# Linear attention with an ELU MLP on one core: the loads of chunks 12 and 13 placed behind the decay work of chunks 10 and 11, and three second products placed between the first products of chunk 8

## The chip, the core and the metric

The kernel runs on one core of one Trainium2 chip. The metric is device time in microseconds (us). Three runs of the kernel before gave 218.0, 218.4 and 217.15 us, so the median is 218.0 us.

The engines are TensorE (PE in the profile, PEld for its weight loads), VectorE (DVE), ScalarE (ACT), GpSimd (POOL) and SyncE (SP). DMAs in this kernel are issued from two queues: POOL issues the input loads, which turn float32 in memory into float16 on chip, and SP issues the transposes and the stores of the result. Both kinds of transfer run on the same 16 DMA engines of the core.

## The reference

There are two parts. The first is causal linear attention with a decay for each head, on q, k, v of shape 4 x 8 x 768 x 64 (batch, heads, tokens, head size), computed block after block with a state that is carried on:

```
intra = (qb @ kb^T * Dmask) @ vb                  # inside the block, masked with lam^(i-j)
inter = (qb * lam^(i+1)) @ kv_state               # from the blocks before
out   = intra + inter
kv_state = lam^block * kv_state + (kb * lam^(block-1-j))^T @ vb
```

The result is laid out as x of 3072 tokens x 512. The second part is an MLP: `h = x @ w_in` (512 x 2048), `g = h if h > 0 else exp(min(h, 0)) - 1`, `y = g @ w_out` (2048 x 512). The output y is float32.

## The kernel before

**Chunks.** The kernel uses blocks of 128 tokens instead of the reference's 64. A chunk is 128 tokens of one batch; there are 24, and chunk g belongs to batch g mod 4 and block g div 4. Chunks 0 to 3 go through the MLP one at a time, the others in pairs (4 and 5, 6 and 7, and so on). Everything that belongs to a pair is named by its first chunk: first product 1:8:j works on chunks 8 and 9 together.

**The steps of a chunk**, by the letters that the written-out order uses:

- `L` (load_pair, line 509) issues three loads on POOL's queue for a pair, in the order q, k, v (line 97). The tiles have four buffers.
- `W` (pool_work, line 513) issues two DMA transposes on SP's queue, q first and k second (line 256, from chunk 8 on; the tiles qT and kT have five buffers). It also does the decay work on POOL: kd, the decayed keys (line 162), and two halves of stt, the old state times its decay (line 366), for which the state update of four chunks earlier must have ended.
- `T` is the transpose on TensorE that chunks 0 to 7 use.
- `S` computes the scores psS on TensorE from kT and qT (line 290), 8 matmuls a chunk; VectorE then multiplies by the mask (pp, line 306).
- `B` is a burst on TensorE for a pair: P, the attention output psO (lines 326 and 332), and U, the addition to the state psU (line 394). VectorE or ScalarE copies the output out as xt (line 349 or 347), and VectorE updates the state st (line 406).
- `1:g:j` is a first product of the MLP, 8 matmuls into one of two psH buffers (line 466). ScalarE computes e = exp(psH) (line 472) and relu in place (line 473), and VectorE joins them as g (line 445). When that join has ended, the psH buffer is free.
- `2:g:j` is a second product, 4 matmuls into psM (line 488). After the fourth one of a chunk, ScalarE copies psM to osb (line 503) and SP's queue stores it (line 438).

**The order.** Nothing is scheduled by a planner: each engine runs its instructions in the order in which the program emits them, and each queue issues its transfers in that order. The emission order is the string OPEN (line 51) for the first part. From the point where OPEN ends, the loop at line 593 goes on by itself: it puts a first product, then the attention steps that are due by the table AT (line 61), then up to two second products that are ready. Any step that OPEN already holds is left out of the loop, so a longer OPEN takes work out of the loop and puts it elsewhere; nothing is done twice.

The VectorE join of a first product is not emitted directly behind it but at the start of the next first or second product (flush, line 440), and one waiting piece of VectorE work (a mask multiplication, a copy, a state update) is emitted behind each flush.

The stores of finished chunks are emitted at the start of first products, and one is kept back each time (line 457). A store waits on SP for its copy, and transposes that come later in SP's order stand behind it.

Of the kernel before, what the change touches and what calls it, by code (L numbers as in the profile page):

```python
# [15 lines left out]
def kernel(  # L16
# [13 lines left out]
    B, H, S, D = q.shape  # L30
# [23 lines left out]
        "2:1:2 1:1:3 U1 1:2:3 M Z3 2:2:2 1:3:2 U2 1:3:1 2:1:3 1:0:3 T5 T4 2:2:3 1:3:3 S4:5 "  # L54
        "2:0:3 2:3:2 2:3:0 M U3 M B:P4:P5:U4:U5 W8 2:3:3 1:4:1 T6 W9 1:4:0 T7 2:3:1 1:4:3 S6:7 "
        "1:4:2 2:4:0 2:5:0 1:4:5 1:4:4 2:4:1 B:P6:P7:U6:U7 1:4:7 1:6:1 2:5:2 2:5:1 1:6:0 1:4:6 "
        "2:4:2 S8:9 1:6:2 1:6:3 2:4:3 2:5:3 L12 1:6:4 B:P8:P9:U8:U9 1:6:5 W11 1:6:6 2:6:0 "
        "2:6:1 W10 1:6:7 2:6:2"
    )
    LAGU = 7  # L60
    AT = {"L": -18, "W": -13, "T": -9, "S": -8, "B": -4}
# [577 lines left out]
```

## Time and profile before

| | |
|---|---|
| median of three runs | 218.0 us (217.15 to 218.4) |
| span of the profiled execution | 215.9 us |
| TensorE busy | 199.9 us, 93% of the span |
| VectorE, ScalarE, GpSimd busy | 129.9, 129.1, 96.2 us |
| input and weight loads (POOL's queue) | 79760 packets, 13.50 MB |
| transposes and stores (SP's queue) | 22192 packets, 10.76 MB |

The whole time of the profiled execution itself is not given beside its span. The span is 2.1 us below the median of the three runs, and 1.2 to 2.5 us below single runs.

How to read it: a "busy" share says how long an engine had something to do, not whether it set the end. The "chain that ended last" goes back from the last instruction, at each step to whatever released it. The list of waits says which engine stood still, for whom, how long in all, how many times, and the longest. A timeline line gives the start, the busy time, the engine, the line of the kernel, the operation and tiles, how many instructions were merged, and in square brackets the idle time ahead of them and what ended it. "SPq" in a timeline is the issue on SP's queue; the time from issue to landing is in the DMA view, as the last number of a line.

### The profile page before, as it was taken

To read this page: it belongs to the slowest core of one execution; us is meant where nothing else is said; L and a number is where in the kernel's file an instruction comes from. 1 tells how busy PE (TensorE), PEld (TensorE's weight loads), DVE (VectorE), ACT (ScalarE), POOL (GpSimd) and SP (SyncE) were. 2 spreads that over 40 slices of the span, in tenths; PEclk is the share of its full clock that TensorE was granted. 3 is DMA by queue.
4 is the path that set the end of the run, shared out by engine and by line. 5 is a ranking of instruction groups with operands and counts; after the bars stand their busy time and mean duration, and the time that the engine had idled before them with its cause. 6 is when DMAs were issued, how large, how long until landed. Compare 5 with 4: busy or idle time off the path is not lost.

```text
span 215.9 us, 5095 instructions
## 1 busy us (share of the span) xinstructions
PE 199.9 (93%) x2036; PEld 138.2 (64%) x2036; DVE 129.9 (60%) x223; ACT 129.1 (60%) x245; POOL 96.2 (45%) x115
## 2 busy tenths in 40 slices
PE   0568999999999998999999999999999999999992
PEld 0466676768685675666766766766766666766641
DVE  3926463777837778658657657667667547444410
ACT  4536664884866656665565566476476576566730
POOL 7998890999996419167067159300000000000000
PEclk9999999999999999999999999999999999999999
DMA  8999999999999956989969919999114110111021
GB/s 89 140 173 193 190 144 180 139 169 144 151 156 145 143 126 131 123 109 97 153 114 125 175 58 103 152 181 152 50 59 90 52 49 0 55 49 49 3 92 54
DMA packets 101976, 24.59 MB, mean 114 GB/s; under 512 B 92608, under 2 KB 99008, under 8 KB 101952
## 3 DMA queue, kind: packets, MB, share of 16 engines
q0 software_dynamic: 79760, 13.50, 82.6%
q1 hardware_dynamic: 22192, 10.76, 25.6%
q8 instruction: 16, 0.26, 0.5%
q14 instruction: 8, 0.07, 0.1%
HBM read 27.27 MB, written 6.29 MB: 155 GB/s over the span
## 4 chain that ended last, share of the span: by engine, by line
PE 83%; DMA 7%; POOL 6%; issue 1%; DVE 1%; ACT 0%; SPq 0%; POOLq 0%
PE psM L488 38%; PE psH L466 36%; DMA wo<-in_moe_w_out_dram 4%; DMA kT<-kn 3%; PE psO L326 3%; PE psS L290 3%; PE psO L332 2%; POOL wi L136 1%; POOL kn L97 1%; POOL vn L97 1%; POOL qn L97 1%; PE psT L271 1%; PE psU L394 1%; POOL kd L162 0%; POOL wo L143 0%
## 5 line engine op out<-in xcount | busy, mean ns | idle before, releaser
L466 PE MATMUL psH<-xt,wi 128*128 128x256 f16 (+1 forms) x896 | 99.9, 259 | 1.5 <-DVE g L445 0.8
L445 DVE SCALAR_TENSOR_TENSOR g<-e,psH 128x512 f16<-128x512 f32 x96 | 65.8, 686 | 56.5 <-ACT psH L473 55.9
L488 PE MATMUL psM<-wo,g 128*128 128x512 f16 (+1 forms) x388 | 96.4, 377 | 0.9 <-DVE osb L501 0.5
L472 ACT ACTIVATE e<-psH 128x512 f32<-128x512 f32 x96 | 57.3, 597 | 66.1 <-PE psH L466 62.8
L466 PEld LDWEIGHTS <-wi 128*128 128x128 f16 x896 | 77.8, 99 | 26.8 <-DVE g L445 2.0
L473 ACT ACTIVATE psH<-psH 128x512 f32<-128x512 f32 x96 | 57.0, 594 | 0.0
L488 PEld LDWEIGHTS <-g 128*128 128x128 f16 x388 | 36.3, 98 | 29.9 <-issue 1.3
L306 DVE TENSOR_TENSOR pp<-psS,mask 128x512 f16<-128x512 f32 x48 | 30.9, 684 | 5.3 <-PE psS L290 5.3
L162 POOL TENSOR_TENSOR kd<-kn,ks 128x512 f16<-128x512 f16 x20 | 20.7, 1039 | 18.7 <-DMA kn<-in_k_dram 17.7
L366 POOL TENSOR_TENSOR stt<-st,upp 64x256 f32<-64x256 f16 x32 | 19.5, 608 | 19.8 <-DVE st L406 13.5
L503 ACT COPY osb<-psM 128x512 f32<-128x512 f32 (+1 forms) x24 | 13.9, 581 | 6.3 <-PE psM L488 6.3
L97 POOL DMA_DIRECT2D kn<-in_k_dram x14 | 15.5, 1106 | 0.8 <-POOLq L623 0.8
L97 POOL DMA_DIRECT2D vn<-in_v_dram x14 | 15.5, 1109 | 0.6 <-DMA wi<-in_moe_w_in_dram 0.6
L326 PE MATMUL psO<-pp,vn 128*64 128x128 f16 x192 | 12.4, 230 | 3.0 <-DMA vn<-in_v_dram 2.9
L97 POOL DMA_DIRECT2D qn<-in_q_dram x13 | 14.8, 1139 | 0.0
L406 DVE TENSOR_TENSOR st<-stt,psU 64x256 f16<-64x256 f32 x32 | 13.3, 417 | 1.2 <-PE psU L394 0.5
L326 PEld LDWEIGHTS <-vn 128*64 128x64 f16 x192 | 10.1, 114 | 6.1 <-DMA vn<-in_v_dram 3.1
L349 DVE TENSOR_TENSOR xt<-psO,qs 128x512 f16<-128x512 f32 x16 | 11.0, 688 | 4.1 <-PE psO L332 4.1
L332 PE MATMUL psO<-qT,st 128*64 128x128 f16 x160 | 10.0, 219 | 0.0
L271 PE MATMUL psT<-ident,qn 128*128 128x128 f16 x32 | 3.8, 252 | 6.5 <-DVE qn L115 5.6
L290 PE MATMUL psS<-qT,kT 64*128 64x128 f16 x192 | 8.7, 228 | 0.8 <-DMA kT<-kn 0.7
L332 PEld LDWEIGHTS <-st 128*64 128x64 f16 x160 | 8.9, 110 | 0.0
(38 smaller groups left out, 64.8 us busy)
## 6 DMA issues: line engine op xcount, KB each, us to landing
out_dram<-osb SPq DMA_DIRECT2D x23, 256.0 KB, 2.5
kn<-in_k_dram POOLq DMA_DIRECT2D x10, 256.0 KB, 8.1
qn<-in_q_dram POOLq DMA_DIRECT2D x10, 256.0 KB, 7.1
vn<-in_v_dram POOLq DMA_DIRECT2D x10, 256.0 KB, 8.6
wi<-in_moe_w_in_dram POOLq DMA_DIRECT2D x8, 256.0 KB, 7.4
wo<-in_moe_w_out_dram POOLq DMA_DIRECT2D x8, 256.0 KB, 8.4
kn<-in_k_dram POOLq DMA_DIRECT2D x4, 128.0 KB, 4.3
vn<-in_v_dram POOLq DMA_DIRECT2D x4, 128.0 KB, 6.1
```

The costliest lines, as they stand in the source:

```text
L97: nc.gpsimd.dma_start(out=t[:].rearrange("p b h d -> p (b h) d"), in_=src)
L162: nc.gpsimd.tensor_tensor(out=kd[:], in0=of(kg, g), in1=ks[:].unsqueeze(2).broadcast_to([128, H, 64]), op=ALU.mult,)
L290: nc.tensor.matmul(psS[g][hh][:, hp, :], lhsT=kt[r, hp, :], rhs=qt[r, hp, :], start=True, stop=True,)
L306: nc.vector.tensor_tensor(out=P[:], in0=pts[hh][:], in1=mask[:, hh::2, :], op=ALU.mult)
L326: nc.tensor.matmul(po[r, hp, :], lhsT=vt[:, 2 * hp + hh, :], rhs=Pt[(g, hh)][:, hp, :], start=True, stop=(cb == 0), skip_group_check=True,)
L332: nc.tensor.matmul(po[r, hp, :], lhsT=st[b][cb % 2][:, hp, r], rhs=qt[:, hp, :], start=False, stop=True, skip_group_check=True,)
L366: nc.gpsimd.tensor_tensor(out=tmp[r], in0=old[r, :, r], in1=upp[r].unsqueeze(2).broadcast_to([64, NHP, 64]), op=ALU.mult,)
L445: nc.vector.scalar_tensor_tensor(out=g[:].rearrange("p f c t -> p (f c t)"), in0=e[:], scalar=-1.0, in1=r[:], op0=ALU.add, op1=ALU.min,)
L466: nc.tensor.matmul(pH[:, f * n * 128 : (f + 1) * n * 128], lhsT=wi16[i][:, kk, w * 128 : (w + 1) * 128], rhs=xg[g0][:, kk, :], start=(kk = ...
L472: nc.scalar.activation(e[:], pH[:], AF.Exp)
L473: nc.scalar.activation(pH[:], pH[:], AF.Relu)
L488: nc.tensor.matmul(psM[g][:, cols], lhsT=gts[(g, j * FB + f)], rhs=wo16[i][:, w, cols], start=first and f == 0, stop=end and f == FB - 1, ...
```

## The change

The order string OPEN gets another end. `L12`, the three loads for chunks 12 and 13, moves from before 1:6:4 to behind `W10`. The string is also longer by seven steps, which the loop had placed before: 1:8:0, S10:11, 2:6:3, 1:8:1, 2:7:0, 1:8:2 and 2:7:1.

```
-        "2:4:2 S8:9 1:6:2 1:6:3 2:4:3 2:5:3 L12 1:6:4 B:P8:P9:U8:U9 1:6:5 W11 1:6:6 2:6:0 "
-        "2:6:1 W10 1:6:7 2:6:2"
+        "2:4:2 S8:9 1:6:2 1:6:3 2:4:3 2:5:3 1:6:4 B:P8:P9:U8:U9 1:6:5 W11 1:6:6 2:6:0 "
+        "2:6:1 W10 L12 1:6:7 2:6:2 1:8:0 S10:11 2:6:3 1:8:1 2:7:0 1:8:2 2:7:1"
```

With the part that the loop adds, the order of the stretch is, before and after (up to 1:8:7; all that follows is the same in both):

```
before: 2:5:3 L12 1:6:4 B8:9 1:6:5 W11 1:6:6 2:6:0 2:6:1 W10 1:6:7 2:6:2 1:8:0 S10:11
        1:8:1 1:8:2 2:6:3 1:8:3 W12 2:7:0 1:8:4 B10:11 2:7:1 1:8:5 W13 2:7:2 1:8:6 L14 2:7:3 1:8:7
after:  2:5:3 1:6:4 B8:9 1:6:5 W11 1:6:6 2:6:0 2:6:1 W10 L12 1:6:7 2:6:2 1:8:0 S10:11
        2:6:3 1:8:1 2:7:0 1:8:2 2:7:1 1:8:3 W12 1:8:4 B10:11 1:8:5 W13 2:7:2 1:8:6 L14 2:7:3 1:8:7
```

On POOL's queue this puts the loads of q, k, v behind kd and stt of chunks 11 and 10, where they stood ahead of them. On SP's queue the order of transposes and stores of chunks up to 13 stays as it was. On VectorE the second mask multiplication of chunk 11 and the join of 1:8:1 change places. On ScalarE the copy of chunk 6's result stands ahead of the exponential of 1:8:1, where it stood behind the relu of 1:8:2.

## The prediction

> **What bounds the kernel now.** I read the shares of busy time first, then the chain that ended last, then TensorE's timeline around the edit, then the timelines of the two queues.
>
> ```profile
> PE 199.9 (93%) x2036; PEld 138.2 (64%) x2036; DVE 129.9 (60%) x223; ACT 129.1 (60%) x245; POOL 96.2 (45%) x115
> ...
> PEclk9999999999999999999999999999999999999999
> ...
> PE 83%; DMA 7%; POOL 6%; issue 1%; DVE 1%; ACT 0%; SPq 0%; POOLq 0%
> ```
>
> TensorE sets the end, at a granted clock that stays in the top tenth. From 70 us on it is nearly never idle, so a change of order can only win what is left of idle time there. Its timeline shows two gaps in the stretch that the edit touches:
>
> ```profile
> 69.26 0.40 PE L290 MATMUL psS<-qT,kT 64*128 64x128 f16 x8
> 70.35 0.40 PE L290 MATMUL psS<-qT,kT 64*128 64x128 f16 x8 [0.70 <-DMA kT<-kn]
> ...
> 82.59 0.62 PE L290 MATMUL psS<-qT,kT 64*128 64x128 f16 x16
> 83.14 1.05 PE L466 MATMUL psH<-xt,wi 128*128 128x256 f16 x8
> 84.96 1.05 PE L466 MATMUL psH<-xt,wi 128*128 128x256 f16 x8 [0.77 <-DVE g L445]
> 85.85 1.03 PE L488 MATMUL psM<-wo,g 128*128 128x512 f16 x4
> ```
>
> The first gap is S9 waiting for the transpose kT9. The second is 1:8:2 waiting for a psH buffer, that of 1:8:0, whose join stands on VectorE behind two mask multiplications of S10:11. The edit aims at both. Now the queues, POOL first and then SP:
>
> ```profile
> 62.02 1.21 POOL L97 DMA_DIRECT2D qn<-in_q_dram  x1
> ...
> 65.58 1.04 POOL L162 TENSOR_TENSOR kd<-kn,ks 128x512 f16<-128x512 f16 x1
> 68.07 1.29 POOL L366 TENSOR_TENSOR stt<-st,upp 64x256 f32<-64x256 f16 x2 [1.45 <-DVE st L406]
> 69.44 1.04 POOL L162 TENSOR_TENSOR kd<-kn,ks 128x512 f16<-128x512 f16 x1
> 70.44 1.29 POOL L366 TENSOR_TENSOR stt<-st,upp 64x256 f32<-64x256 f16 x2
> ```
>
> ```profile
> 64.93 9.86 SPq L438 DMA_DIRECT2D out_dram<-osb  x3
> 74.96 1.23 SPq L256 DMA_TRANSPOSE qT<-qn  x1
> 76.28 1.22 SPq L256 DMA_TRANSPOSE kT<-kn  x1
> 77.61 1.21 SPq L256 DMA_TRANSPOSE qT<-qn  x1
> 78.87 1.26 SPq L256 DMA_TRANSPOSE kT<-kn  x1
> ```
>
> The last four are chunk 11's and then chunk 10's transposes, held back by a store that waits for ScalarE's copy (73.83). The line to watch is kT10, issued last at 78.87 and needed by S10 at 82.6. What a transpose takes from issue to landing is in the DMA view; first the answer for 74.8 to 79 us, with no loads in flight, then one for 101.4 us, amid the loads of chunk 16:
>
> ```profile
> qT<-qn SPq DMA_TRANSPOSE x2, 2.4
> kT<-kn SPq DMA_TRANSPOSE x2, 2.5
> ```
>
> ```profile
> vn<-in_v_dram POOLq DMA_DIRECT2D x1, 256.0 KB, 10.2
> kT<-kn SPq DMA_TRANSPOSE x1, 7.7
> ```
>
> So a transpose lands in 2.4 us alone, and in about 7 among loads. Transposes issued beside loads, from about 1 us after the first load of a group, read: kT9 6.9, kT13 7.0, qT15 7.8, kT15 7.7, qT17 6.4, kT17 6.9, qT19 7.2, kT19 7.7; median 7.1.
>
> **The change, part by part.**
>
> *S9's wait goes.* S8 starts at 69.26 and eight matmuls of this kind take 0.28 (16 of them take 0.55 at 82.59), so S9 could start at 69.54; it starts at 70.35: 0.81 us lost. kT9 was issued at 63.45, among L12's loads (62.02 to 65.5), and took 6.9. Without them the only other transfers are stores; an earlier transpose, kT8 at 59.29, took 4.5 with the tail of older loads beside it. At 4.5 kT9 lands at 67.95, ahead of the need. Next late for S9 would be qT9, issued before it. Gain 0.81; the bounds are 0 (kT9 still late) and 0.81. I take 0.81.
>
> *1:8:2's wait goes.* 1:8:1 starts at 83.14 and takes 0.87 in the chain, so 1:8:2 could start at 84.01 but starts at 84.96: 0.95. With 2:6:3 ahead of 1:8:1 and 2:7:0 behind it, two second products of 0.86 each lie between, more than the wait. Gain 0.95, and the second products only change place, so TensorE's work stays the same.
>
> *A new wait at 1:8:4.* Those second products now lack further on: 1:8:2, 2:7:1, 1:8:3, 1:8:4 follow one another. A psH buffer comes free 3.0 us after its product began (1:8:2 began at 84.96, its join ran 87.23 to 87.92, and a released product starts 0.04 later). 1:8:4 comes 0.87 + 0.86 + 0.87 = 2.60 behind 1:8:2 and needs its buffer: 0.38 lost. Its bounds are 0 (were the buffer free 13% sooner) and 0.95, the like wait of before; the chain from product to join is the same three steps, so I take 0.38. 1:8:5 follows the burst of 1.3 us, so it is covered; if the cover went, it would miss by the same 0.4.
>
> *L12 behind W10.* On POOL, kd11 now runs in the place of the loads, but stt11 still waits for VectorE's state update until 68.07; kd10 and stt10 follow and end at 71.73. So L12 is issued from 71.7 to 75.2 instead of 62.0 to 65.5. SP's queue: the store's copy comes 0.81 earlier, so qT11, kT11, qT10, kT10 are issued from 74.15, 75.45, 76.8 and 78.05, all inside L12's transfer (qT10 takes the buffer of qT8, which P8 reads until about 75, so that holds nothing up). A group's last load landed 10.8 to 12.7 us after the group's first issue (v14 86.21 + 8.5 against 83.87; v20 132.19 + 10.4 against 129.86): L12 is in flight until 82.5 to 84.4. S10 is reached at 82.66 - 0.81 = 81.85.
>
> When does kT10 land? Alone 78.05 + 2.4 = 80.5, so no wait; at the worst row, 78.05 + 7.8 = 85.85, a wait of 4.0. No row has a transpose issued so late in a load group, with three others ahead on its queue. The median row gives 85.15; the drain of the loads at its latest gives 84.4. I take 84.7, between them, as the loads thin out near the end: S10 waits 2.85 us. S11's transposes were issued earlier, and are no longer late by then. DVE's mask work behind S10 starts later with it, but TensorE is the one late.
>
> *Queued behind.* kd12 now waits for kn12 (71.7 + 1.2 + 8.0 = 80.9; it ran at 71.81), then stt12, kd13, stt13 (4.7 us in all) put L14 at 85.6 to 86.5 instead of 83.87. SP's kT12 waits for the same load instead of going at 82.22; with 7.8 for each landing, kT13 is there by 95, against S12 at 97.7. L14's two us pass on to kd14 (92.97 before) and L16 (98.01), and end in the next group, where POOL waited 1.95 for VectorE. No cost: the cover is that kd14 and kd15 are used only in the burst at 105; without it each us there is one on TensorE.
>
> **Sum:** -0.81 - 0.95 + 0.38 + 2.85 = +1.47 us. The profiled span of 215.9 becomes 217.4; around it lie 2.1 us to the median of the runs (1.2 to 2.5 to single ones), whose whole time for this very execution isn't given. On the median: 219.5.
>
> [...] TensorE stood idle for 2.87 us before 12.70 and the clock in the windows 10 to 14 and 14 to 18 us stayed 1.00. [...]
>
> Transposes beside loads took three times their time alone (7.1 against 2.4). [...]
>
> **Rivals.**
>
> 1. *Transposes of chunk 10 come in time (other side).* L12 is spread, and its first data flow only 2 us after the issue. If kT10 lands within 3.8 us of its issue (by 81.85), no wait takes the place of the old ones: -0.81 - 0.95 + 0.38 = -1.38, 216.6 us. For it: kT16, 3.0, was issued just ahead of a load group, and qT13 took 4.9. Against it: no transpose amid loads took under 6.4.
> 2. *In between.* kT10 lands at 82.1 to 84.3, as the loads run dry: wait 0.3 to 2.4, sum -1.1 to +1.1, about 218.0 us.
> 3. *The gain of S9 doesn't come:* kT9 was late for the store issued at 64.93 or its own slow start, not for L12. Then +0.81 on the forecast, 220.3. Against it: qT11 to kT10 landed in 2.4 with a store ahead of them.
>
> **How the numbers follow.** A measurement of this kernel tells about 0.5% (1.1 us) from no change. Late transposes (the forecast, wait over 2.46): 0.50, and rival 3, also slower: 0.08. In between: 0.22. In time: 0.20. So slower 0.58, same 0.22, faster 0.20. The likeliest case's own range is 219.1 to 220.7 (wait 2.46 to 4.0). The range of 8 in 10 reaches down into the rivals, to 216.8, which leaves out about half of the in-time case, and up to 220.8, for a wait at the worst row.
>
> **What would show it.** In the changed profile: S8 and S9 as one group of 16 matmuls with no gap; no wait of 1:8:2; a gap of 0.4 before 1:8:4 released by VectorE's g; loads of chunk 12 issued at 71.7; transposes issued 74.2 to 78.1 with landings near 7; a gap of 2 to 4 us before S10 released by kT; nothing new after. The prediction is wrong if the landing stays under 4, if the loads move elsewhere than 71.7, or if TensorE's gaps after 90 us exist.

## The result and the profile after

The changed kernel takes 219.69 us (median of 21 runs, 217.84 to 221.35), the kernel before 218.76 us in the runs beside it (217.0 to 223.66). The ratio is 1.0061 with a 95% interval of 1.0038 to 1.0084: slower by 0.6%. The forecast was 219.5 us against 218.0, a ratio of 1.007.

Runs far above their kernel's fastest are left out of the ratio, and in 52 later runs of the kernel before these are just the nine with a granted clock of 0.992 or less (median span 219.0 us, against 216.1 in the others), while in the changed kernel twelve of 21 runs have such a clock and eleven of them are counted. Over all 21 runs of each, the medians are only 0.4% apart.

The page of the changed kernel, first lines of its busy times and of its slices, in which TensorE's clock and TensorE's busy tenths dip in one and the same place:

```profile
span 218.5 us, 5095 instructions
...
PE 200.9 (92%) x2036; PEld 138.5 (63%) x2036; DVE 129.8 (59%) x223; ACT 129.2 (59%) x245; POOL 96.2 (44%) x115
...
PE   0568999999999996999999999999999999999992
...
PEclk9999999999999996999999999999999999999998
```

TensorE's timeline in the stretch of the edit (S8 and S9; 1:8:0, S10:11, 2:6:3, 1:8:1; 1:8:4):

```profile
69.35 0.62 PE L290 MATMUL psS<-qT,kT 64*128 64x128 f16 x16
...
80.84 1.04 PE L466 MATMUL psH<-xt,wi 128*128 128x256 f16 x8
84.08 1.03 PE L290 MATMUL psS<-qT,kT 64*128 64x128 f16 x16 [2.20 <-DMA kT<-kn]
85.05 1.89 PE L488 MATMUL psM<-wo,g 128*128 128x512 f16 x4
86.73 1.42 PE L466 MATMUL psH<-xt,wi 128*128 128x256 f16 x8
...
91.84 1.03 PE L466 MATMUL psH<-xt,wi 128*128 128x256 f16 x8 [0.22 <-DVE g L445]
```

S8 and S9 are one group now: the wait for kT9 is gone. So is the wait of 1:8:2. In their place S10 stands still for kT10, and 1:8:4 waits a little for its psH buffer. Behind S10 the work itself is slow: 16 score matmuls take 0.97 us to the next start instead of 0.55, and 2:6:3 and 1:8:1 together 2.94 (85.05 to 87.99) instead of 1.73. The table of stretches says why; its columns are the stretch, its length, the busy time of PE, PEld, DVE, ACT and POOL (with the number of instructions in brackets), the granted clock, the DMA share and GB/s:

```profile
83.00:84.00 1.00, 0.00 (x0) 0.00 (x0) 0.00 (x0) 0.06 (x1) 0.98 (x1) 1.00 1.20 355
84.00:85.00 1.00, 0.92 (x16) 0.77 (x16) 0.28 (x1) 0.00 (x0) 0.93 (x3) 0.55 1.21 269
85.00:86.00 1.00, 1.00 (x7) 0.41 (x4) 1.00 (x3) 0.00 (x0) 1.00 (x2) 0.50 0.68 130
86.00:87.00 1.00, 1.00 (x5) 0.39 (x4) 1.00 (x3) 0.03 (x1) 1.00 (x2) 0.50 1.73 128
87.00:88.00 1.00, 1.00 (x9) 0.80 (x8) 0.80 (x2) 0.56 (x1) 1.00 (x2) 0.75 0.50 18
88.00:89.00 1.00, 1.00 (x8) 0.52 (x6) 0.00 (x0) 0.75 (x2) 0.76 (x1) 1.00 2.33 137
```

For some 3.4 us behind the wait (84.1 to 87.5 us) TensorE was granted half its clock, 0.50. Why kT10 was late stands in the timelines of POOL's queue, of SP's queue, and in the landings of qT11 and of kT10 (the DMA view of 74 to 75 and of 79 to 80 us):

```profile
71.76 1.20 POOL L97 DMA_DIRECT2D qn<-in_q_dram  x1
72.96 1.15 POOL L97 DMA_DIRECT2D kn<-in_k_dram  x1
74.09 1.16 POOL L97 DMA_DIRECT2D vn<-in_v_dram  x1
```

```profile
74.18 1.51 SPq L256 DMA_TRANSPOSE qT<-qn  x1
75.78 2.01 SPq L256 DMA_TRANSPOSE kT<-kn  x1
77.89 1.28 SPq L256 DMA_TRANSPOSE qT<-qn  x1
79.23 1.26 SPq L256 DMA_TRANSPOSE kT<-kn  x1
```

```profile
qT<-qn SPq DMA_TRANSPOSE x1, 7.7
...
kT<-kn SPq DMA_TRANSPOSE x1, 4.8
```

The loads are issued from 71.76, the last of them lands at 83.09 (74.09 + 9.0), and all four transposes are issued in between. 79.23 + 4.8 = 84.03 us is when kT10 lands; S10 starts 0.05 later. From 76.5 to 78.5 us the loads moved 1683 packets and SP's queue 220; by what resource the loads hold the transposes up is not shown by any run here.

The account from the start of S8 to the start of S12, which lies behind all that the edit touches: before 69.26 to 97.73, 28.47 us; after 69.35 to 100.26, 30.91 us; +2.44. It is made of -0.87 (S8 to 1:6:2: 1.42 before, 0.55 after), +2.27 (1:8:0 to S10: 0.97, then 3.24), +0.42 (the scores at the lower clock), -0.95 (1:8:2), +0.38 (1:8:4: 90.59 + 0.87 to 91.84) and +1.20 (2:6:3 and 1:8:1 at the lower clock). The sum is 2.45. The whole span grew by 2.6; of the rest, 0.09 us lie ahead of S8 and 0.07 behind the start of S12.

The clock does not fall in every run. In the 21 runs the granted clock is 0.997 to 0.999 in nine, with a median span of 216.7 us, and 0.984 to 0.992 in twelve, with 218.35: 1.65 us apart, about the 0.42 + 1.20 us of the profile. Where the clock fell in the other eleven is not known, since only one run has a profile.

### The profile page after: what moved, and what is told of

Same layout as the page of the kernel before. It is cut to its first block, busy times and chain, and to the rows that moved or that the text cites. A ratio compares the mean times of both kernels' runs of the same rounds, so it can differ in the third digit from the quotient of the medians.

```text
span 218.5 us, 5095 instructions
## 1 busy us (share of the span) xinstructions
PE 200.9 (92%) x2036; PEld 138.5 (63%) x2036; DVE 129.8 (59%) x223; ACT 129.2 (59%) x245; POOL 96.2 (44%) x115
## 4 chain that ended last, share of the span: by engine, by line
PE 77%; DMA 10%; POOL 7%; SPq 2%; issue 1%; ACT 1%; DVE 1%; POOLq 0%; ACTq 0%
PE psM L488 35%; PE psH L466 33%; DMA wi<-in_moe_w_in_dram 4%; DMA wo<-in_moe_w_out_dram 4%; PE psS L290 3%; PE psO L326 3%; DMA kT<-kn 2%; PE psO L332 2%; SPq L256 2%; POOL kd L162 1%; POOL wi L136 1%; POOL kn L97 1%; POOL vn L97 1%; PE psT L271 1%; PE psU L394 1%
## 5 line engine op out<-in xcount | busy, mean ns | idle before, releaser
L488 PE MATMUL psM<-wo,g 128*128 128x512 f16 (+1 forms) x388 | 97.6, 380 | 1.1 <-DVE osb L501 0.5
L290 PEld LDWEIGHTS <-kT 64*128 64x128 f16 x192 | 6.0, 100 | 5.4 <-DMA kT<-kn 2.5
```

Source lines behind the costliest of these rows:

```text
L290: nc.tensor.matmul(psS[g][hh][:, hp, :], lhsT=kt[r, hp, :], rhs=qt[r, hp, :], start=True, stop=True,)
L488: nc.tensor.matmul(psM[g][:, cols], lhsT=gts[(g, j * FB + f)], rhs=wo16[i][:, w, cols], start=first and f == 0, stop=end and f == FB - 1, ...
```

## The experiments

The theory: the loads of chunk 12 and 13, where the change puts them, delay the transposes of chunk 10; S10's wait for these is more than the two waits that go; and a wait of that size (2.20 us in the profile) can cost a second time through the clock (1.62 us there). The rivals: the new places of the second products do the harm; or S10 waits for something else than the loads.

Each kernel's stretch from S8 to S12 can be compared across runs free of the start-up, so it stands beside the ratio below. It is that of the one profiled run of each; the ratio is that of all runs, to the kernel before.

**The loads alone.** Only L12 moves:

```
-  2:5:3 L12 1:6:4 ... W10 1:6:7 2:6:2"
+  2:5:3 1:6:4 ... W10 L12 1:6:7 2:6:2"
```

> Only the loads of chunks 12 and 13 move behind the decay work of chunks 10 and 11; the second products stay where they were before. Theory (late transposes): S9's wait goes (-0.8 us), S10 waits 2 to 2.5 us for kT10, and where TensorE's clock falls to half behind that wait 1.8 us more are lost; 1:8:2's wait of 0.95 stays, since its cause is the VectorE work of S10:11. Sum +1.4 without the clock's fall, +3.2 with it, so a ratio of 1.006 to 1.015. Rival (the new places of the second products do the harm): at or under the time of before, with -0.8 from S9.

Ratio 1.0079 (1.0047 to 1.0111), stretch 30.28 us. TensorE's timeline:

```profile
69.28 0.62 PE L290 MATMUL psS<-qT,kT 64*128 64x128 f16 x16
...
84.42 0.62 PE L290 MATMUL psS<-qT,kT 64*128 64x128 f16 x16 [2.61 <-DMA kT<-kn]
84.97 1.05 PE L466 MATMUL psH<-xt,wi 128*128 128x256 f16 x8
86.79 1.05 PE L466 MATMUL psH<-xt,wi 128*128 128x256 f16 x8 [0.77 <-DVE g L445]
```

The loads by themselves make the kernel slower, at a full clock here (1.00 from 80 to 90 us; the scores take 0.55 again): -0.87 for S9 and +2.68 for S10 give the 1.81 us that the stretch gained. The wait of 1:8:2 stays, as expected. The clock fell in 7 of 12 runs (granted clock 0.990 to 0.992), but there it cost only 0.4 us (median spans 218.0 and 217.6), not the 1.8 that was expected: a lower clock lengthens the work ahead of 1:8:2, which had 0.95 us of waiting to give. That last step is argued, not shown.

**The second products alone.** L12 in its old place, the new tail of OPEN:

```
-  2:6:1 W10 1:6:7 2:6:2"
+  2:6:1 W10 1:6:7 2:6:2 1:8:0 S10:11 2:6:3 1:8:1 2:7:0 1:8:2 2:7:1"
```

> Only the three second products move; the loads stay ahead of the decay work. Theory: 1:8:2's wait of 0.95 goes, 1:8:4 waits 0.4, S9's wait of 0.8 stays, transposes of chunk 10 land in 2.4 us as before, S10 doesn't wait: -0.6 us, ratio 0.997. Rival (the new places of the second products do the harm): slower than before by 0.5% or more.

Ratio 0.9991 (0.9953 to 1.003). That rules out the rival's harm of 0.5%; the gain of 0.6 us itself is too small for it. The profile fell on the longest of the twelve runs, which shows something else:

```profile
69.48 0.40 PE L290 MATMUL psS<-qT,kT 64*128 64x128 f16 x8
72.39 0.40 PE L290 MATMUL psS<-qT,kT 64*128 64x128 f16 x8 [2.52 <-DMA kT<-kn]
72.72 3.33 PE L466 MATMUL psH<-xt,wi 128*128 128x256 f16 x16
...
92.45 1.03 PE L466 MATMUL psH<-xt,wi 128*128 128x256 f16 x8 [0.22 <-DVE g L445]
```

With the loads in the old place, kT9 took 7.9 us to land in this run and S9 waited 2.5, after which the clock fell (0.52 and 0.50 in the stretches 73 to 75 us). The stretch is 31.40 us. Without S9's lost time (69.76 to 72.39, 2.63) and the slow work (3.13 and 2.03 instead of 1.76 and 1.73, so 1.67) 27.10 remain; before, without S9's 0.81, it is 27.66. The difference, -0.56, is what the second products bring: 0.95 less at 1:8:2 and 0.38 more at 1:8:4.

**The loads some 3 us sooner** (issued from 68.90 instead of 71.76), between the decay work of chunk 11 and that of chunk 10:

```
-  1:6:5 W11 1:6:6 2:6:0 2:6:1 W10 L12 1:6:7
+  1:6:5 W11 L12 1:6:6 2:6:0 2:6:1 W10 1:6:7
```

> The changed kernel, but with the loads between the decay work of chunk 11 and that of chunk 10, so issued from 69.4 instead of 71.8 us. Theory: the loads drain 2.3 us sooner, by about 81; kT10 then lands at 81.5 to 82.5 instead of 84.0, S10 waits 0 to 0.7 instead of 2.3, too short for the clock to fall: -0.7 to -1.4 against before, ratio 0.994 to 0.997. Rival (any load behind the state update of chunk 7 makes the transposes late by the whole of 7 us): S10 waits as in the changed kernel, ratio 1.006.

Ratio 0.9908 (0.9875 to 0.9941), stretch 27.04 us, 1.43 less than before.

```profile
68.86 0.62 PE L290 MATMUL psS<-qT,kT 64*128 64x128 f16 x16
...
81.32 0.62 PE L290 MATMUL psS<-qT,kT 64*128 64x128 f16 x16
81.88 1.04 PE L488 MATMUL psM<-wo,g 128*128 128x512 f16 x4
```

S10 does not wait, so how short a wait leaves the clock alone is not shown here; the granted clock was 0.995 or more in all nine runs. kT10, issued at 78.11, landed after 3.2 us, at 81.3, just as S10 came. In order of issue the four transposes took 6.1, 5.1, 4.0 and 3.2 us, with the loads issued from 68.90: the same transposes get faster as the loads run dry (1099 packets of theirs from 75 to 76 us, 77 from 77.7 to 78.7). All of what the change lost hangs on 2.9 us in when the loads are issued.

**The decay work split.** kd11 and kd10, then the loads, then the four halves of stt:

```
-  2:5:3 1:6:4 ... W11 ... W10 L12
+  2:5:3 K11 K10 L12 1:6:4 ... W11 ... W10
   # K is att_kd alone; pool_work leaves out a kd or stt that is there already
```

> The changed kernel, but POOL does kd11 and kd10 first, then the three loads, then the four halves of stt, which wait for the state update. The loads are issued from about 64.3 us. Theory: kT9, issued at 64.2, has its data moved before the first load's data flow 2 us after its issue, so S9 doesn't wait (at worst 0.8 as before); the loads have drained by 75 to 76 and the transposes of chunks 11 and 10 land in 2.4 to 4, so S10 doesn't wait: -1.4 us against before, ratio 0.994. Rival (S10's wait has another cause than the loads): S10 waits about 2 us here too.

Ratio 0.9904 (0.9874 to 0.9933), stretch 70.70 to 97.73, 27.03 us; neither S9 nor S10 waits. Its one wait in the stretch is that of 1:8:4:

```profile
70.70 0.62 PE L290 MATMUL psS<-qT,kT 64*128 64x128 f16 x16
...
83.16 0.62 PE L290 MATMUL psS<-qT,kT 64*128 64x128 f16 x16
...
89.31 1.03 PE L466 MATMUL psH<-xt,wi 128*128 128x256 f16 x8 [0.22 <-DVE g L445]
```

**The loads still later**, behind stt12, which waits for a state update at 79 us:

```
-  W10 L12 1:6:7
+  W10 N12 L12 1:6:7
   # N is att_M, the two halves of stt, alone
```

> The changed kernel, but the two halves of stt12, which wait for the state update of chunk 8 at 79 to 80 us, stand ahead of the loads, so these are issued from about 80.7. Theory: the transposes of chunks 11 and 10 run with no loads beside them, land in 2.4 us each, and S10 doesn't wait: 1.4 us less than before up to there. Then the transposes of chunks 12 and 13 come late, since their data land at 86 to 90: S12 and S13 (96.5) may wait 0 to 3. Rival (S10's wait comes from the store ahead of the transposes or from SP's issue, not from the loads): S10 waits about 2 us here too.

Ratio 0.9928 (0.9894 to 0.9962), stretch 69.14 to 96.18, 27.04 us. With the loads issued from 80.45, the four transposes landed in 2.4, 2.4, 2.4 and 2.5 us. SP's timeline, where they are all issued before that:

```profile
73.97 1.23 SPq L256 DMA_TRANSPOSE qT<-qn  x1
75.29 1.23 SPq L256 DMA_TRANSPOSE kT<-kn  x1
76.63 1.22 SPq L256 DMA_TRANSPOSE qT<-qn  x1
77.90 1.26 SPq L256 DMA_TRANSPOSE kT<-kn  x1
```

The store ahead of them is as in the changed kernel, and the first transpose goes out at the same time (73.97, there 74.18), so the rival falls: it is the loads. SP's issue of a transpose, too, is back at 1.22 to 1.26 us, where kT11 took 2.01 in the changed kernel. The wait of 0 to 3 us that I allowed S12 did not come.

**The wait filled.** The loads as in the change, two second products ahead of S10:11:

```
-  1:8:0 S10:11 2:6:3 1:8:1 2:7:0 1:8:2 2:7:1"
+  1:8:0 2:6:3 2:7:0 S10:11 1:8:1 2:7:1 1:8:2"
```

> The changed kernel with the loads where it has them, but 2:6:3 and 2:7:0 ahead of S10:11 instead of behind it, so TensorE has 1.73 us of work while kT10 is under way. Theory: S10's wait falls from 2.2-2.6 to 0.5-0.9, TensorE's clock stays full, and 1:8:3 waits up to 0.4 for its psH buffer in place of 1:8:4: from S8 to S12 about 27.6 us against 28.5 before and 30.9 in the changed kernel's profile; ratio 0.995 to 0.998. Rival (the clock falls for another reason than the idle time at S10): it falls in half of the runs here too, and the median is above that of before.

Ratio 0.9997 (0.9968 to 1.0025); stretch 69.69 to 97.90, 28.21 us.

```profile
82.05 1.89 PE L488 MATMUL psM<-wo,g 128*128 128x512 f16 x8
84.19 0.62 PE L290 MATMUL psS<-qT,kT 64*128 64x128 f16 x16 [0.24 <-DMA kT<-kn]
...
87.74 1.03 PE L466 MATMUL psH<-xt,wi 128*128 128x256 f16 x8 [0.22 <-DVE g L445]
89.48 1.03 PE L466 MATMUL psH<-xt,wi 128*128 128x256 f16 x8 [0.70 <-DVE g L445]
```

S10's wait is nearly gone and the clock held in all 12 runs (0.997 to 1.0). I missed 0.6 us: with no second product left between 1:8:2 and 1:8:4, both 1:8:3 and 1:8:4 wait for psH (0.38 and 0.87 us lost).

**One place each.** The split decay work, and each of the three second products moved by only one place:

```
-  1:8:0 S10:11 2:6:3 1:8:1 2:7:0 1:8:2 2:7:1"
+  1:8:0 S10:11 1:8:1 2:6:3 1:8:2 2:7:0 1:8:3 W12 2:7:1"
```

> The loads as in the run with the split decay work, and the three second products moved by one place each only (2:6:3 behind 1:8:1, 2:7:0 behind 1:8:2, 2:7:1 ahead of 1:8:4). Theory: S9 and S10 don't wait, 1:8:2 waits 0.1, and 1:8:4 has two second products between itself and 1:8:2 again (3.5 us against the 3.0 that a psH buffer needs), so its wait of 0.22 to 0.4 goes: the stretch from S8 to S12 falls from 27.04 to 26.7 to 26.8 us. Rival (the wait of 1:8:4 doesn't come from the lack of a second product): it stays, and the stretch stays at 27.0.

Stretch 69.25 to 95.98, 26.73 us; ratio 0.9907 (0.9871 to 0.9942), median 215.67 us against 218.25.

```profile
82.26 1.05 PE L466 MATMUL psH<-xt,wi 128*128 128x256 f16 x8
83.14 1.03 PE L488 MATMUL psM<-wo,g 128*128 128x512 f16 x4
84.08 1.05 PE L466 MATMUL psH<-xt,wi 128*128 128x256 f16 x8
...
87.56 1.04 PE L466 MATMUL psH<-xt,wi 128*128 128x256 f16 x8
```

No line of the stretch has a wait left: 1:8:2 starts 0.07 late (83.14 + 0.87 = 84.01), 1:8:4 (87.56) on time. By the stretch this is the best of the kernels; by the ratio it can't be told from the other two with early loads. All three are 0.9% faster than the kernel before, and so faster than the changed one.

**The kernel before once more.**

> The kernel before, for another profile. Theory: S9's wait for kT9 varies from run to run (0.7 us in the first profile, 2.5 in the run with the second products alone, where the loads stand at the same place), and when it is near 2 us or more the clock falls behind it, so the kernel before loses more there on average than its first profile showed. Rival: the wait is 0.7 us again and the clock stays.

```profile
68.41 0.40 PE L290 MATMUL psS<-qT,kT 64*128 64x128 f16 x8
70.47 0.40 PE L290 MATMUL psS<-qT,kT 64*128 64x128 f16 x8 [1.65 <-DMA kT<-kn]
```

S9's wait was 1.65 us here, against 0.70 in the first profile and 2.52 with the second products alone; the clock stayed at 1.00. The third of these is another kernel, but the same up to this place. So a single profile gave the size of this wait at its low end. Of the changed kernel there is only the one profile, with the lower clock; its runs with a full clock are known by their spans alone. That the clock falls when the wait is near 2 us or more is not what the runs show: with the loads alone it held after 2.61 us.

## Why the prediction was right

*The chain.* The forecast named the mechanism and its place: L12, put behind stt11's wait, is issued from 71.7 (71.76 measured), the transposes of chunks 11 and 10 fall among it, and S10 waits. The runs with the loads alone, sooner, and later show that the place of the loads decides this, and nothing else in the edit.

*S9's gain.* Taken as 0.81; 0.87 measured. kT9, taken at 4.5 us, landed in 2.5 without the loads beside it. But the gain is against a profile with a short wait; three profiles with the loads in the old place show 0.70, 1.65 and 2.52. On average the gain is larger, which the early-load kernels show: with the loads between, or the decay work split, the stretch is 1.4 us shorter than in the first profile of before, but the median time is shorter by 2.1 to 2.3 us, and the median span of the runs with a full clock by 1.8 to 2.0.

*1:8:2 and 1:8:4.* -0.95 and +0.38, measured the same to 0.01 us. Of the reasons, the 3.0 us from a first product's start to the release of its buffer held in each kernel where 1:8:4 waited (2.99 in all of them), and giving 1:8:4 a second product more took its wait away.

*S10's wait.* The term of 2.85 was a little too high: 2.27 in the profile, 2.68 with the loads alone. It was right for two errors that nearly cancel. I had SP issue kT10 at 78.05; amid the loads the issue of kT11 took 2.01 us instead of 1.22 and kT10 went out at 79.23. I had it land 6.65 us later; it took 4.8, with the loads running dry (960 packets of theirs from 80 to 81 us, 167 from 81 to 82, 41 from 82 to 82.5). The guess that it lands about when the loads end held, 0.9 us behind the last load. The prediction says that no row has a transpose issued so late in a load group with three others ahead, and that none amid loads took under 6.4 us. The profile before does have such rows, further on than its timelines were read: four transposes on SP's queue at 144.25, 145.60, 146.90 and 148.55, the first three issued before the last load of a group landed at 147.59, took 6.1, 5.2, 5.0 and 3.8 us. With 5.0 to 5.2 in place of 6.65 the wait would have been put at 1.2 to 1.4 us, and the sum at about zero.

*The clock.* The sum has no term for a lower clock; from an idle time of 2.87 us with a clock of 1.00 I took it that the clock would hold. That failed: it fell in 12 of 21 runs (granted clock 0.984 to 0.992) and cost 1.62 us in the profile, 1.65 between the two groups of spans. There 2.2 us of idle time came ahead of it, and the half clock lasted from 84.1 to 87.5 us. Nor does the profile before show a clock that held there, since the work on both sides of the idle time is slow:

```profile
8.48 1.35 PE L290 MATMUL psS<-qT,kT 64*128 64x128 f16 x16
12.70 1.06 PE L326 MATMUL psO<-pp,vn 128*64 128x128 f16 x16 [2.87 <-DMA vn<-in_v_dram]
...
16.37 0.61 PE L290 MATMUL psS<-qT,kT 64*128 64x128 f16 x8
```

A score matmul took 0.304 us on average at 8.48 and at 16.37, against 0.217 at 82.59; in the changed kernel, at half the clock, it took 0.306 (84.08). So the 1.00 that the table of stretches gives for 14 to 18 us does not fit the times of the matmuls at 16.37.

*So the time was right in part by luck, by parts that offset one another.* With the full clock the stretch would be 0.8 us longer than before (2.44 less 1.62), 0.4% of the time, where the sum had 1.47; the median spans of the runs with a full clock, 216.7 and 216.1, are 0.6 apart. The fall of the clock in over half of the runs, which the sum left out, lifts it, and S9's larger gain takes some of it back; how much each gives on average is argued, not shown. The forecast of +1.5 us and the measured 0.61% of 218 us, 1.3 us, agree more closely than the terms do.

*Rival 1* (transposes in time) and *rival 3* (S9's gain doesn't come) are out: kT10 took 4.8 us, over the 3.8 of rival 1, and S9 doesn't wait. *Rival 2* (the wait about offsets the gains) is, by its own conditions, what the profile shows: kT10 landed at 84.03 (82.1 to 84.3 was its bound) after a wait of 2.27 (0.3 to 2.4), below the 2.46 that the forecast asked for. Its time of about 218.0 didn't come, since the clock fell; with the loads alone the wait was 2.68, so it lies on either side of the limit.

*L14 and what follows.* L14 went out at 85.25 instead of 83.87, L16 at 101.03 instead of 98.01, with no wait of TensorE for a load or a transpose behind it, as predicted: from 90 us on it waits 0.2 us at 1:8:4 and 0.5 for a copy to osb, the second as in the kernel before.

## What to carry to other kernels

In these runs a group of loads delayed the short transposes beside it for as long as it lasted: some 11 us in the changed kernel (71.76 to 83.09), where the four took 4.8 to 7.7 us against 2.4 and 2.5 with no loads beside them. So place the loads by the deadline of the short transfers beside them, not only by the deadline of their own data. Moving a load out of the way of one transfer is worth nothing until it is checked which transfer it now meets. And where a profile shows a wait for a transfer amid others, take its size from several runs: S9's wait here was 0.70, 1.65 and 2.52 us in three.

## What was not expected

Idle time of TensorE and the fall of its clock are not tied by length alone in these runs. The clock fell after 2.20 us (the changed kernel) and 2.52 us (second products alone), and held after 2.61 us (loads alone) and 1.65 us (the kernel before once more). In the five kernels without a long wait in this stretch (three with early loads, one with later loads, one with the wait filled) it fell in none of 48 runs (granted clock 0.995 or more); with the wait it fell in 12 of 21 and 7 of 12. What decides it is not shown by any run here.

The time of a transpose from issue to landing ran from 2.4 us (the run with the loads still later) to 8.0 us (qT11 and kT11 in the run with the loads alone). For the four transposes of chunks 11 and 10 it fell in the order of issue, with less and less of the load group still to come: 7.7, 7.7, 5.8, 4.8 in the changed kernel, and 8.0, 8.0, 6.8, 5.9 with the loads alone. There the last load landed at 83.53, and the last three transposes 0.2 to 0.9 us behind it.
